# Attention: the third maximum of a step in two 256-key parts, and a bank and an exponential for each score

## The chip, the cores and the metric

The kernel runs on one core of a Trainium2 chip. The time is the device time of one launch in microseconds (us). Three runs of the kernel before gave 3602.53, 3603.29 and 3605.42 us (median 3603.29). A core has TensorE for matmuls (PE in the profile, its weight loads PEld), VectorE (DVE), ScalarE (ACT), GpSimd (POOL) and queues that issue DMAs (SP). Matmuls write to a small memory of eight banks of 512 fp32 columns on 128 partitions (PSUM), which VectorE and ScalarE read.

## The reference

Four sublayers follow each other on x of 2048 tokens by 512: Fourier mixing, attention, Fourier mixing, attention, each on a layer norm of x and added to x. The change lies in the attention:

```python
q = (x @ wq).reshape(B, S, 32, 16).transpose(0, 2, 1, 3)
k = x @ wk                      # one key head of 16 for all 32 query heads
v = x @ wv
scores = einsum("bhqd,bkd->bhqk", q, k) * 16 ** -0.5
p = softmax(scores)
o = einsum("bhqk,bkd->bhqd", p, v)
x = x + o.transpose(0, 2, 1, 3).reshape(B, S, 512) @ wo
```

## The kernel before

**Phases.** A layer has a phase A (Fourier mixing, projections of q, k and v, and some of the maxima early, one after the other between its matmuls) and a phase B (attention and output projection). Phase A of the first layer ends about 644 us into the span and phase B runs to 1801; the second layer's run to 2433 and 3589.

**Rows in halves.** A query or key has 48 rows of values in split precision and rows for the maximum; with padding 64 partitions. Two head groups, g = 0 on partitions 0 to 63 and g = 1 on 64 to 127, share each tile. TensorE is split in two groups of 64 rows, and a matmul of the one can run beside one of the other.

**Phase B** has 512 steps: 16 tiles of 128 queries (`i`), each in 32 steps (`s_`), which are two halves of the heads by 16 chunks of 128 keys. A step does the following.

- `pv` (L910): the probabilities of two steps ago times the values, four matmuls into the one bank z, each on 32 columns of the array and all 128 rows. In the profile these are eight records.
- `score` (L896): four matmuls, j = 0 to 3, g = j mod 2, each 128 keys by 512 (four heads of 128 queries). Two of them fill the two banks of a tile x, and one exponential of 1024 columns (L899) reads both. There are two tiles x, four banks. In the last steps of a layer, when no maxima are left, scores 2 and 3 go to single banks y (L889, L891).
- `max_half` (its matmul shows as L78, its reduce as L102): the softmax needs the maximum of each query and head ahead of its tile's turn. One unit is 128 queries of one head against 512 keys into a bank y, from which VectorE takes one maximum into `mxp`. Units come in the order of (tile, head pair, 512 keys, g), so that g alternates. `owed` holds the pace at three units a step, and twelve ahead.

The banks are z (one), y (three) and x (four). A matmul that takes a bank y waits for the reduce of an earlier one.

**Order.** The program's order is the order on each engine; nothing reorders it. In a step the first unit's g decides: score 1-g, a maximum of g, score g, maxima of 1-g and of g, score 3-g, score 2+g. So one row group gets four matmuls of 512 columns in a step and the other three, and in the next step the other way round. Scores wait for the exponential that read their banks, maxima for the reduces.

**Around it.** Five steps ahead of need, `max_neg` reduces a tile's partial maxima `mxp` (four per head) to `nm`, `max_split` splits it into `ms`, and `max_rows` transposes it and writes it to the rows of q. `out_tasks` and `half_tasks` store, normalise and project the tile before: step 12 of each tile has twelve 128-row matmuls (`o_proj`), and VectorE adds x to the result (L976).

Of the kernel before, what the change touches and what calls it, by code (L numbers as in the profile page):

```python
# [8 lines left out]
F32 = mybir.dt.float32  # L9
# [38 lines left out]
def fnet_mqa_kernel(ctx: ExitStack, tc: tile.TileContext, x_in, ct, dt_, wq, wkv, wo, out):  # L48
# [6 lines left out]
    def f(ap):  # L55
        return ap.bitcast(F32)

# [62 lines left out]

    def pair():
        return ps.tile([P, 2, 512], F32, name="x", bufs=2)
# [127 lines left out]
    def make_layer(L, src, mid, dst, last):  # L250
# [201 lines left out]
        def max_neg(i, p0=0, n=NPAIR, k=4, whole=False):  # L452
            nm = sb.tile([P, NPAIR, 2], F32, name="nm")[:, :n, :]
            vec.tensor_reduce(nm, o.mxp[i][:, p0:p0 + n, :, :k], op=ALU.max, axis=AX.X, negate=True)
            if p0 + n == NPAIR:
                o.mxp.pop(i)
            st["nm"] = nm
            if whole:
                max_split()

        def max_split():
            nmv = st.pop("nm").rearrange("p a g -> p g a")
            n = nmv.shape[2]
            ms = sb.tile([P, 2, 2, NPAIR], F32, name="ms").rearrange("p g r a -> p (g r a)")
            ms = ms[:, :4 * n].rearrange("p (g r a) -> p g r a", g=2, r=2)
# [173 lines left out]
        def phase_a(extra):  # L639
            tasks = {}  # L640
            Pace.pe = Pace.dve = Pace.act = Pace.pool = 0.0
# [212 lines left out]
            units.extend((0, pr, g, 3) for pr in range(HALF, NPAIR) for g in range(2))  # L854
            units.extend((i, pr, g, kb) for i in range(1, NT) for pr in range(NPAIR) for kb in range(4) for g in range(2)
                         if pr >= taken.get((i, kb), 0))
            max_neg(0, 0, HALF, 5, True)
            for k in range(12):
                more_max()
                if k == 2:  # L860
                    max_rows(0, 0, HALF, nc.scalar)

        units = []
        o.done = o.extra = 0

        def more_max():
            if o.done < len(units) and units[o.done][0] in o.loaded | {0}:
                max_half(*units[o.done])
                o.done += 1

        def owed(n):
            return min(3 * (n + 1) + 12 + o.extra, len(units)) - o.done

        def done_with(i, pr):
            return all(u[:2] > (i, pr) for u in units[o.done:])
# [3 lines left out]
        def score(i, s_, j):  # L879
# [6 lines left out]
            w = j // 2  # L886
            if i == NT - 1 and jj == 1 and o.done == len(units):
# [5 lines left out]
            first = "e" not in st  # L893
            if first:
                st["e"] = pair()
            nc.tensor.matmul(st["e"][:, g, :], kz[64 * g:64 * g + KR, c * P:(c + 1) * P],  # L896
                             o.qT[i][64 * g:64 * g + KR, cp:cp + 4, :], start=True, stop=True)
            if not first:
                nc.scalar.activation(ptiles[i, s_][:, 2 * w:2 * w + 2, :], st.pop("e"), AF.Exp, scale=DH ** -0.5)  # L899
# [65 lines left out]
        def o_proj(i):  # L965
            for k in range(NK):
                o_mm(k)
                if k == NK - 1:
                    o_add(i)
                if k % 2 and 3 <= i < NT - 1:  # L970
                    for _ in range(2):
                        more_max()
                        o.extra += 1
# [64 lines left out]
        def phase_b(nxt):  # L1038
# [9 lines left out]
            behind = []  # L1048
            for n in range(NT * NSTEP):
# [4 lines left out]
                g = units[o.done][2] if o.done < len(units) else 1  # L1054
                for j, m in ((1 - g, 1), (g, 2), (3 - g, 0), (2 + g, 1)):
                    score(i, s_, j)
                    for _ in range(m):
                        if owed(n) >= 1:
                            more_max()
# [16 lines left out]
                for at, j, p0, np_ in ((NT - AHEAD, i, HALF, HALF), (NSTEP - AHEAD, i + 1, 0, HALF if i == NT - 2 else NPAIR)):  # L1076
                    if j in (0, NT - 1) or j == i + 1 < NT:
                        if s_ == at:
                            assert done_with(j, p0 + np_ - 1), (n, j, o.done, len(units), units[o.done], owed(n))
# [3 lines left out]
                        if s_ == at + 2:  # L1083
                            max_rows(j, p0, np_)
            if nxt is not None:
# [70 lines left out]
```

## Time and profile before

| what | value |
|---|---|
| runs (us) | 3602.53, 3603.29, 3605.42 |
| the profiled execution's own time | 3602.02 us |
| its span | 3600.2 us |
| granted TensorE clock | 0.997 |
| phase B, layer 1 and 2 | 1157 and 1156 us |
| phase B, busy of 1157.18 us | PE 1150.76, DVE 975.60, ACT 1002.46, POOL 168.10 |

A row of a timeline gives start, length (of all merged instructions together), engine, line, operation, tiles and, in brackets, the idle time before and what ended it. The chain of waits in order of time has start, length and what the end waited on. A group of instructions has line, engine, operation, out<-in, count, busy us, mean ns of one, and idle time with what ended it. A length is from issue to result, so neighbouring instructions of one engine overlap: their spacing, not their length, is what they cost in a row. PE ends are modelled.

### The profile page before, as it was taken

What the parts mean: (1) busy time and instruction counts of PE and PEld (TensorE: products, weight loads), DVE (VectorE), ACT (ScalarE), POOL (GpSimd) and SP (SyncE); (2) the same over time, 40 slices, a digit from 0 to 9 for tenths busy, and PEclk for the clock granted to TensorE, in tenths of its full rate; (3) what the DMA queues carried; (4) which work ended last, traced back from release to release, by engine and by line L of the source; (5) the groups of instructions that cost most, each with busy time, mean ns of one, the idle gap of its engine ahead of it and who ended that gap; (6) DMA issues with size and microseconds to landing.
All of it is one profiled execution on the core that took longest, in us unless ns stands there. A gap on an engine that the chain in (4) does not pass through costs nothing.

```text
span 3600.2 us, 63751 instructions
## 1 busy us (share of the span) xinstructions
PE 3551.6 (99%) x25090; PEld 1901.3 (53%) x25090; DVE 2801.6 (78%) x4819; ACT 2390.8 (66%) x3050; POOL 781.9 (22%) x976
## 2 busy tenths in 40 slices
PE   8999999999999999999999999999999999999999
PEld 6787877434333433343377878773433343333433
DVE  6186987888888888888311979878888888888882
ACT  4323232888888888888933232229888888888888
POOL 5544342011211111111264343420000000000000
PEclk9999999999999999999999999999999999999999
DMA  5544242211111100110144343422111111011100
GB/s 181 140 140 134 99 137 60 75 49 37 34 32 51 34 23 22 49 34 25 40 141 113 128 118 106 130 60 86 34 35 34 50 35 34 22 29 43 35 24 25
DMA packets 204445, 240.85 MB, mean 67 GB/s; under 512 B 36848, under 2 KB 160752, under 8 KB 197232
## 3 DMA queue, kind: packets, MB, share of 16 engines
q1 hardware_dynamic: 199216, 219.98, 20.5%
q0 software_dynamic: 4864, 16.78, 1.6%
q8 instruction: 196, 3.21, 0.4%
q14 instruction: 105, 0.86, 0.1%
q10 hardware_dynamic: 64, 0.02, 0.0%
HBM read 172.48 MB, written 63.17 MB: 65 GB/s over the span
## 4 chain that ended last, share of the span: by engine, by line
PE 85%; DVE 7%; ACT 2%; issue 1%; DMA 1%; SPq 0%; POOL 0%; DVEq 0%; ACTq 0%; POOLq 0%
PE z L910 27%; PE y L78 19%; PE x L896 19%; PE x L78 17%; DVE mxp L102 4%; PE z L78 1%; DVE mxe L102 1%; ACT slot L899 1%; PE z L83 1%; ACT slot L891 0%; PE y L889 0%; DVE row L102 0%; DVE bst L102 0%; DVE ms L102 0%; PE y L83 0%
## 5 line engine op out<-in xcount | busy, mean ns | idle before, releaser
L102 DVE TENSOR_REDUCE mxp<-y 128x1 f32<-128x512 f32 (+1 forms) x3472 | 2166.7, 679 | 267.3 <-PE y L78 218.1
L899 ACT ACTIVATE slot<-x 128x1024 f32<-128x1024 f32 x1992 | 1943.4, 1027 | 313.6 <-PE x L896 226.4
L910 PE MATMUL z<-slot,v 128*32 128x512 f32 x8192 | 1096.4, 605 | 1.7 <-ACT row L913 1.7
L78 PE MATMUL y<-kz,slot 64*128 64x512 f32 (+1 forms) x3048 | 980.1, 424 | 4.4 <-DVE kz L102 2.1
L896 PE MATMUL x<-slot,kz 64*128 64x512 f32 x2960 | 891.2, 447 | 0.8 <-DMA slot<-mt 0.8
L896 PEld LDWEIGHTS x<-slot,kz 64*128 64x128 f32 x2960 | 368.1, 185 | 734.3 <-ACT slot L899 599.7
L78 PEld LDWEIGHTS y<-kz,slot 64*128 64x128 f32 x3048 | 487.8, 185 | 121.8 <-DVE mxp L102 26.5
L78 PE MATMUL x<-ch,xnh 64*128 64x512 f32 (+2 forms) x2048 | 531.6, 372 | 11.7 <-ACT xnh L102 9.5
L78 PE MATMUL x<-ch,xnl 64*128 64x512 f32 (+2 forms) x2048 | 527.8, 364 | 1.0 <-POOL xnl L102 0.6
L78 PE MATMUL x<-cl,xnh 64*128 64x512 f32 (+2 forms) x2048 | 524.3, 364 | 0.4 <-POOL cl L102 0.4
L950 POOL TENSOR_TENSOR row<-row,row 128x256 f32<-128x256 f32 x63 | 46.3, 734 | 1573.7 <-DMA row<-rd 1184.2
L102 POOL TENSOR_TENSOR cl<-craw,ch 128x512 fp32r<-128x512 f32 x244 | 318.0, 1321 | 298.2 <-ACT ch L102 243.0
L78 PEld LDWEIGHTS x<-ch,xnh 64*128 64x128 f32 (+1 forms) x2048 | 293.1, 185 | 63.4 <-issue 16.2
L78 PEld LDWEIGHTS x<-ch,xnl 64*128 64x128 f32 (+1 forms) x2048 | 298.7, 185 | 38.0 <-POOL xnl L102 4.4
L78 PEld LDWEIGHTS x<-cl,xnh 64*128 64x128 f32 (+1 forms) x2048 | 295.0, 185 | 32.2 <-POOL cl L102 0.7
L910 PEld LDWEIGHTS z<-slot,v 128*32 128x32 f32 x8192 | 163.7, 108 | 274.6 <-issue 247.5
L102 ACT COPY junk<-x 128x2 f32<-128x2 f32 x236 | 37.7, 160 | 350.6 <-PE x L78 328.0
L102 DVE TENSOR_REDUCE mxe<-y 128x1 f32<-128x512 f32 x408 | 257.1, 679 | 9.8 <-PE y L78 9.6
L102 ACT CAST ch<-craw 128x512 fp32r<-128x512 f32 x264 | 158.8, 620 | 155.7 <-PE x L78 120.2
L78 PE MATMUL y<-slot,slot 128*128 128x512 f32 x816 | 216.4, 406 | 8.2 <-DVE mxp L102 6.7
L78 PEld LDWEIGHTS y<-slot,slot 128*128 128x128 f32 x816 | 144.7, 188 | 63.1 <-issue 28.2
L896 PE MATMUL x<-xnl,kz 64*128 64x512 f32 x512 | 154.5, 443 | 0.3 <-DMA xnl<-mt 0.3
(126 smaller groups left out, 2576.9 us busy)
## 6 DMA issues: line engine op xcount, KB each, us to landing
craw<-ct_in SPq DMA_DIRECT2D x112, 512.0 KB
slot<-qd SPq DMA_DIRECT2D x42, 1024.0 KB
qd<-row SPq DMA_DIRECT2D x144, 128.0 KB
od<-row SPq DMA_DIRECT2D x252, 64.0 KB
row<-x_in SPq DMA_DIRECT2D x32, 256.0 KB
mid<-row POOLq DMA_DIRECT2D x32, 256.0 KB, 2.6
craw<-ct_in SPq DMA_DIRECT2D x32, 256.0 KB
row<-mid SPq DMA_DIRECT2D x32, 256.0 KB
```

Source lines behind the costliest of these rows:

```text
L78: nc.tensor.matmul(out_, w, x, **k)
L83: nc.tensor.transpose(out_, x, i_)
L102: return fn(out_, in_, *a, **k)
L896: nc.tensor.matmul(st["e"][:, g, :], kz[64 * g:64 * g + KR, c * P:(c + 1) * P], o.qT[i][64 * g:64 * g + KR, cp:cp + 4, :], start=True, sto ...
L899: nc.scalar.activation(ptiles[i, s_][:, 2 * w:2 * w + 2, :], st.pop("e"), AF.Exp, scale=DH ** -0.5)
L910: nc.tensor.matmul(a[32 * j:32 * j + 32, :], v1[:, c, :], pt[:, j, :], start=c == 0, stop=c == NT - 1)
L950: nc.gpsimd.tensor_mul(bt["ot"][:, cs], bt["ot"][:, cs], bt["den"][:, cs])
```

## The change

- A step takes two "whole" units as before (g = 0 and g = 1 of the same 512 keys) and a "couple" in place of a third unit: 256 keys for both g, in the two halves of one y bank. The couple's matmul for g = 0 ("half 0") is the first of the step behind `pv`, that for g = 1 ("half 1") the last. One reduce with two results follows it. A couple exists in 968 of the 1024 steps.
- The two halves write one bank from two row groups, so half 1 waits until half 0 has ended: an empty instruction on ScalarE (`relay`), ahead of score 1's exponential, waits for half 0, and half 1 waits for it.
- Each score has a bank (e0 to e3, one buffer each) and an exponential of 512 columns. Their order is 1, 0, 3, 2, whatever the units are. The four banks are a pool of their own, `scores`, in place of the tiles x, which phase A takes from a pool `pairs`.
- `mxp` has six columns instead of four. The couple of the second 256 keys of a set writes to column 4 or 5. A memset on GpSimd sets these at each tile's start.
- `nm` and `ms` live in a row tile that the attention's output also uses.

The diff, cut to its core:

```diff
...
+    def behind_(later, first):
+        tc.add_manual_dep(later.ins, first.ins.name,
+                          mybir.DependencyInfo(mybir.DependencyClass.Sync, mybir.DependencyReason.DATA), reason="row halves")
...
+    class Wide:
+        cm = pool = None
+
+    def wide(name):
+        if Wide.cm:
+            Wide.cm.__exit__(None, None, None)
+        Wide.cm = name and tc.tile_pool(name=name, bufs=1, space=PSUM, reuse_waits="tile")
+        Wide.pool = name and Wide.cm.__enter__()
+
     def pair():
-        return ps.tile([P, 2, 512], F32, name="x", bufs=2)
...
-                o.mxp[i] = sb.tile([P, NPAIR, 2, 4 if i else 5], F32, name=f"mxp{i % 4}")
+                o.mxp[i] = sb.tile([P, NPAIR, 2, 6], F32, name=f"mxp{i % 4}")
+                nc.gpsimd.memset(o.mxp[i][:, HALF if i == 0 else 0:, :, 4:6], -3.0e38)
...
+        def max_whole(i, pr, kb):
+            for g in range(2):
+                max_half(i, pr, g, kb)
+
+        def max_couple(i, pr, kb, h, g):
+            if g == 0:
+                st["couple"] = bank("y").rearrange("p (g c) -> p g c", g=2)
+            gs = slice(64 * g, 64 * g + KR)
+            c0 = 512 * kb + 256 * h
+            m = nc.tensor.matmul(st["couple"][:, g, :], o.qT[i][gs, pr, :], kz[gs, c0:c0 + 256], start=True, stop=True)
+            if g == 0:
+                st["first"] = m
+                return
+            behind_(m, st.pop("relay"))
+            k = kb
+            if h:
+                k = 4 + o.coupled.get((i, pr), 0)
+                o.coupled[i, pr] = k - 3
+                assert k < 6
+            nc.vector.reduce_max(partial(i)[:, pr, :, k], st.pop("couple"), axis=AX.X)
+
+        def relay():
+            st["relay"] = nc.scalar.nop()
+            behind_(st["relay"], st.pop("first"))
...
-        def max_neg(i, p0=0, n=NPAIR, k=4, whole=False):
-            nm = sb.tile([P, NPAIR, 2], F32, name="nm")[:, :n, :]
+        def max_neg(i, p0=0, n=NPAIR, k=6, whole=False):
+            st["gather"] = half(0 if i or p0 else 2)
+            nm = st["gather"][:, 64:64 + 2 * n].rearrange("p (a g) -> p a g", g=2)
...
+        def pick_whole(n):
+            if owed(n) >= 2 and ready():
+                o.done += 2
+                return pairs.pop(0)
+
+        def pick_couple(n):
+            if owed(n) < 1:
+                return None
+            if "rest" in st:
                 o.done += 1
+                return *st.pop("rest"), 1
+            if ready():
+                o.done += 1
+                st["rest"] = pairs.pop(0)
+                return *st["rest"], 0
...
-            first = "e" not in st
-            if first:
-                st["e"] = pair()
-            nc.tensor.matmul(st["e"][:, g, :], kz[64 * g:64 * g + KR, c * P:(c + 1) * P],
+            e = Wide.pool.tile([P, 512], F32, name=f"e{j}")
...
+            if "first" in st:
+                relay()
+            nc.scalar.activation(ptiles[i, s_][:, j, :], e, AF.Exp, scale=DH ** -0.5)
...
+            wide(f"scores{L}")
             for n in range(NT * NSTEP):
                 i, s_ = divmod(n, NSTEP)
                 if len(behind) == 2:
                     pv(*behind.pop(0))
                 behind.append((i, s_))
-                g = units[o.done][2] if o.done < len(units) else 1
-                for j, m in ((1 - g, 1), (g, 2), (3 - g, 0), (2 + g, 1)):
-                    score(i, s_, j)
-                    for _ in range(m):
-                        if owed(n) >= 1:
-                            more_max()
+                whole = pick_whole(n)
+                couple = pick_couple(n)
+                if couple:
+                    max_couple(*couple, 0)
+                score(i, s_, 1)
+                score(i, s_, 0)
+                if whole:
+                    max_whole(*whole)
+                score(i, s_, 3)
+                score(i, s_, 2)
+                if couple:
+                    max_couple(*couple, 1)
```

TensorE, one step in the middle of phase B. Before (`z` is pv, `x` scores, `y` maxima; the second name is what moves or stays: kz the keys, the other the queries; the bracket names the engine waited for):

```order
L910 MATMUL z_14743<-slot6_14958,v1_74 32x512 x4
L896 MATMUL x_15008<-xnh_85,kz_70 128x512 [waits Activation_49]
L78 MATMUL y_15010<-kz_70,slot0_13547 128x512 [waits DVE_49]
L896 MATMUL x_15008<-xnh_85,kz_70 128x512
L78 MATMUL y_15015<-kz_70,slot0_13547 128x512 [waits DVE_49]
L78 MATMUL y_15018<-kz_70,slot0_13547 128x512 [waits DVE_49]
L896 MATMUL x_15021<-xnh_85,kz_70 128x512 [waits Activation_49]
L896 MATMUL x_15021<-xnh_85,kz_70 128x512
```

and of the change:

```order
L969 MATMUL z_18411<-slot6_18645,v1_74 32x512 x4
L464 MATMUL y_18702<-kz_70,slot1_15927 128x256 [waits DVE_49]
L954 MATMUL e1_18705<-slot8_13907,kz_70 128x512 [waits Activation_49]
L954 MATMUL e0_18709<-slot8_13907,kz_70 128x512 [waits Activation_49]
L82 MATMUL y_18712<-kz_70,slot1_15927 128x512 [waits DVE_49]
L82 MATMUL y_18715<-kz_70,slot1_15927 128x512 [waits DVE_49]
L954 MATMUL e3_18718<-slot8_13907,kz_70 128x512 [waits Activation_49]
L954 MATMUL e2_18721<-slot8_13907,kz_70 128x512 [waits Activation_49]
L464 MATMUL y_18702<-kz_70,slot1_15927 128x256 [waits Activation_sequencer_49]
```

The row groups are, in order behind z, before (here g = 0): 1, 0, 0, 1, 0, 1, 0; now 0, 1, 0, 0, 1, 1, 0, 1. The first maximum of a step stood second and is now fifth, behind half 0 and score 0 of its row group. The banks of y, by the wait counts in the program: before, each of a step's three maxima takes the bank of the maximum with the same place in the step before. Now half 0 takes the bank of whole 0 of the step before, whole 0 that of whole 1, and whole 1 (y_18715) that of the couple (y_18673, next rows); the last is so in 930 steps.

VectorE, the reduces of a step. Before:

```order
L102 TENSOR_REDUCE mxp3_14893<-y_15010 128x1 [waits PE_49]
L102 TENSOR_REDUCE mxp3_14893<-y_15015 128x1 [waits PE_49]
L102 TENSOR_REDUCE mxp3_14893<-y_15018 128x1 [waits PE_49]
```

and of the change, two steps:

```order
L106 TENSOR_REDUCE mxp0_17873<-y_18683 128x1 [waits PE_49]
L106 TENSOR_REDUCE mxp0_17873<-y_18686 128x1 [waits PE_49]
L474 TENSOR_REDUCE mxp0_17873<-y_18673 128x2 [waits PE_49]
L106 TENSOR_REDUCE mxp0_17873<-y_18712 128x1 [waits PE_49]
L106 TENSOR_REDUCE mxp0_17873<-y_18715 128x1 [waits PE_49]
L474 TENSOR_REDUCE mxp0_17873<-y_18702 128x2 [waits PE_49]
```

The couple's bank is the first of the step to be written to and the last to be read.

More of the change, by code (lines that the diff above doesn't have):

```diff
@@ L853, in phase_a, with ready, more_pair @@
                 taken[EARLY[e][:2]] = NPAIR - len(left)
-            units.extend((0, pr, g, 3) for pr in range(HALF, NPAIR) for g in range(2))
-            units.extend((i, pr, g, kb) for i in range(1, NT) for pr in range(NPAIR) for kb in range(4) for g in range(2)
+            pairs.extend((0, pr, 3) for pr in range(HALF, NPAIR))
+            pairs.extend((i, pr, kb) for i in range(1, NT) for pr in range(NPAIR) for kb in range(4)
                          if pr >= taken.get((i, kb), 0))
+            o.total = 2 * len(pairs)
             max_neg(0, 0, HALF, 5, True)
-            for k in range(12):
-                more_max()
-                if k == 2:
+            for k in range(6):
+                more_pair()
+                if k == 1:
                     max_rows(0, 0, HALF, nc.scalar)
[L863 to L868, printed above, removed]
-                o.done += 1
+        pairs = []
+        o.done = o.extra = o.total = 0
+        o.coupled = {}
+        def ready():
+            return pairs and pairs[0][0] in o.loaded | {0}
+        def more_pair():
+            if ready():
+                max_whole(*pairs.pop(0))
+                o.done += 2
+        def pick_whole(n):
+            if owed(n) >= 2 and ready():
+                o.done += 2
+                return pairs.pop(0)
[3 more added lines that the diff above has]
+            if "rest" in st:
+                o.done += 1
+                return *st.pop("rest"), 1
+            if ready():
+                o.done += 1
+                st["rest"] = pairs.pop(0)
+                return *st["rest"], 0
         def owed(n):
-            return min(3 * (n + 1) + 12 + o.extra, len(units)) - o.done
+            return min(3 * (n + 1) + 12 + o.extra, o.total) - o.done
         def done_with(i, pr):
-            return all(u[:2] > (i, pr) for u in units[o.done:])
+            return all(u[:2] > (i, pr) for u in pairs + [st[k] for k in ("rest",) if k in st])
         ptiles = {}
@@ L885, in score @@
                 ptiles[i, s_] = slot((6, 7, 2)[k % 3]).rearrange("p (j n) -> p j n", j=4)
-            w = j // 2
-            if i == NT - 1 and jj == 1 and o.done == len(units):
+            if i == NT - 1 and jj == 1 and o.done == o.total:
                 e = bank("y")
@@ L892, in score @@
                 return
-            first = "e" not in st
-            if first:
-                st["e"] = pair()
-            nc.tensor.matmul(st["e"][:, g, :], kz[64 * g:64 * g + KR, c * P:(c + 1) * P],
+            e = Wide.pool.tile([P, 512], F32, name=f"e{j}")
+            nc.tensor.matmul(e, kz[64 * g:64 * g + KR, c * P:(c + 1) * P],
                              o.qT[i][64 * g:64 * g + KR, cp:cp + 4, :], start=True, stop=True)
-            if not first:
-                nc.scalar.activation(ptiles[i, s_][:, 2 * w:2 * w + 2, :], st.pop("e"), AF.Exp, scale=DH ** -0.5)
+            if "first" in st:
+                relay()
+            nc.scalar.activation(ptiles[i, s_][:, j, :], e, AF.Exp, scale=DH ** -0.5)
         acc = {}
@@ L970, in o_proj @@
                 if k % 2 and 3 <= i < NT - 1:
-                    for _ in range(2):
-                        more_max()
-                        o.extra += 1
+                    more_pair()
+                    o.extra += 2
         def o_add(i):
@@ L1084, in phase_b @@
                             max_rows(j, p0, np_)
+            wide(None)
             if nxt is not None:
```

8 lines of the change are left out of this document (4 added, 4 removed).

## The prediction

> **What bounds the kernel now.** I read the page first, then the chain of waits, then single steps on the timeline.
>
> ```profile
> PE 3551.6 (99%) x25090; PEld 1901.3 (53%) x25090; DVE 2801.6 (78%) x4819; ACT 2390.8 (66%) x3050; POOL 781.9 (22%) x976
> PE 85%; DVE 7%; ACT 2%; issue 1%; DMA 1%; SPq 0%; POOL 0%; DVEq 0%; ACTq 0%; POOLq 0%
> ```
>
> TensorE is busy nearly all the time and carries 85% of the chain. The change touches the attention phase only, 1024 steps in two layers. There the chain, seen in order of time, repeats itself:
>
> ```profile
> 1195.62 1.00 PE z L910 x8
> ...
> 1204.12 0.99 PE z L910 x8
> 1205.11 0.42 PE x L896
> 1205.54 0.00 PE y L78
> 1205.54 0.23 PE x L896
> 1205.77 0.23 PE y L78 x2
> 1206.00 0.24 PE x L896
> ...
> 1212.63 1.00 PE z L910 x8
> ```
>
> From 1195.62 to 1212.63 are eight steps: 2.126 us each. In a step the probability-times-value block takes 0.99 us. Then come the 64-row matmuls, about 0.235 us for 512 columns on one half of the array's rows. Both halves work side by side, but there are seven matmuls, so one half gets four of them. The same on the timeline:
>
> ```profile
> 1201.37 1.89 DVE L102 TENSOR_REDUCE mxp<-y 128x1 f32<-128x512 f32 x3 [0.23 <-PE y L78]
> 1202.93 0.49 PE L896 MATMUL x<-slot,kz 64*128 64x512 f32 x1
> 1202.93 0.49 PE L78 MATMUL y<-kz,slot 64*128 64x512 f32 x1
> 1203.26 0.39 PE L896 MATMUL x<-slot,kz 64*128 64x512 f32 x1
> 1203.31 0.18 PEld L78 LDWEIGHTS y<-kz,slot 64*128 64x128 f32 x1
> 1203.49 1.89 DVE L102 TENSOR_REDUCE mxp<-y 128x1 f32<-128x512 f32 x3
> 1203.62 0.18 PEld L896 LDWEIGHTS x<-slot,kz 64*128 64x128 f32 x2
> 1203.62 0.50 PE L896 MATMUL x<-slot,kz 64*128 64x512 f32 x2
> 1203.75 1.94 ACT L899 ACTIVATE slot<-x 128x1024 f32<-128x1024 f32 x2 [0.18 <-PE y L78]
> 1204.05 1.06 PE L910 MATMUL z<-slot,v 128*32 128x512 f32 x8
> 1205.04 0.49 PE L896 MATMUL x<-slot,kz 64*128 64x512 f32 x1
> ```
>
> First score and first maximum start at 1202.93, the next pair at 1203.26: 0.335 us, since the first weight load has no cover (0.10 over the 0.235). Four places on the busier half make 0.335 + 3 x 0.235 = 1.04; the value block starts 1.12 after 1202.93, so the switch costs 0.08. With the block's 0.99 (1204.05 to 1205.04) TensorE alone gives 2.11, and the step is 2.126: TensorE sets it.
>
> Two engines are close behind. ScalarE needs 1.94 for its two exponentials. VectorE reduces three banks in 1.89, the first starting 0.56 after the first maximum's matmul. The y banks number three. The reduces of the step before end at 1201.37 + 1.89 = 1203.26, and the third maximum's weights load at 1203.31. So that maximum comes only just after its bank is free: release to load is 0.05. This circle goes over two steps: last reduce, 0.05, 0.10 for the load, 0.235 for the maximum, 0.235 for the score behind it, 0.08, 0.99, then the first maximum of the next step but one to its reduce 0.56, then 1.89. Sum 4.14, or 2.07 a step, against 2.126. The slack is 0.06 us.
>
> **The change part by part.**
>
> I call the rows 0 to 63 row group 0 and 64 to 127 row group 1; scores 0 and 2, "whole 0" (a maximum over 512 keys) and "half 0" (256 keys) run on the one, scores 1 and 3, "whole 1" and "half 1" on the other. The two halves fill one bank, the couple's, and share a reduce. So in 968 steps the third maximum, 512 columns on one row group, becomes 256 columns on each. Each then has 3.5 places for 4, if whole 1 may start before whole 0: 0.115 us less, 2.01 a step.
>
> VectorE's work: no fewer reduces; the third writes two columns. The trace has no such form, so I take bounds.
>
> ```profile
> L102 DVE TENSOR_REDUCE mxp<-y 128x1 f32<-128x512 f32 x3408 | 2142.3, 684 | 258.1 <-PE y L78 212.8 <-PE x L896 37.3
> L102 DVE TENSOR_REDUCE mxp<-y 128x1 f32<-128x256 f32 x64 | 24.4, 420 | 9.2 <-PE y L78 5.3 <-PE x L78 1.7
> L102 DVE TENSOR_REDUCE nm<-mxp 128x32 f32<-128x128 f32 x28 | 7.7, 276 | 0.0
> ```
>
> Low 684 ns, as one reduce of 512; high 2 x 420 = 840, as two of 256. By 684 and 420, 128 elements into one result would be 288, and 128 into 32 results take 276: a result more costs nothing. I take 684.
>
> **The order of the reduces is where the change loses.** Until now the first reduce belongs to a matmul that starts with the step. Now VectorE's order is whole 0, whole 1, couple, and whole 0 stands behind half 0 and score 0 on its rows: 0.335 - 0.115 + 0.235 = 0.455 into the step. The couple's reduce is last as before, and its bank is given to whole 1 of the next step (in 930 of the 968 steps, by the program's wait counts), wanted 0.335 into it. With TensorE's 2.01: whole 0 starts at 0.455, its reduce at 0.455 + 0.46 (0.56 without the load's 0.10) = 0.915, all three end at 2.805. Whole 1 of the next step could start at 2.345 and comes, 0.05 behind the bank's release, at 2.855: 0.51 late. Scores 3 and 2, half 1 and the value block stand behind it in TensorE's queue. That a waiting matmul holds back what follows, even on idle rows, shows where the other phase puts a pair of maxima between its matmuls:
>
> ```profile
> 2375.58 0.18 PEld L78 LDWEIGHTS y<-kz,slot 64*128 64x128 f32 x1 [0.79 <-DVE kz L102]
> 2376.04 0.18 PEld L78 LDWEIGHTS y<-kz,slot 64*128 64x128 f32 x1 [0.28 <-DVE kz L102]
> 2376.05 0.29 PEld L78 LDWEIGHTS x<-ch,xnh 64*128 64x128 f32 x2
> ```
>
> The second maximum waits for VectorE until 2376.04. The two loads behind it wait for nothing of their own, and the first of them is for the rows that the first maximum had left; they come at 2376.05.
>
> The lateness feeds back, over two steps. From the couple's last reduce: 0.05, whole 1 with its uncovered load 0.335, score 3 0.235, half 1 0.115, the switch 0.08, the block 0.99, then 0.455 to whole 0, 0.46 to its reduce, 1.89 for three. Sum 4.61: **2.305 us a step**, 0.18 over 2.126. Where whole 1's place in the order matters (before or behind whole 0), it is not in this sum: the wait puts it behind anyway.
>
> How many steps: 968, less two each for the 32 output projections, whose twelve extra matmuls let VectorE catch up.
>
> ```profile
> L976 DVE TENSOR_TENSOR row<-y,row 128x512 f32<-128x512 f32 x32 | 22.1, 692 | 70.6 <-PE y L78 56.2 <-issue 14.4
> ```
>
> 904 x 0.18 = 163 us.
>
> ScalarE: four exponentials of 512 for two of 1024. The end of the phase has both kinds:
>
> ```profile
> 3535.29 1.03 ACT L899 ACTIVATE slot<-x 128x1024 f32<-128x1024 f32 x1 [0.51 <-PE x L896]
> 3536.21 1.08 ACT L891 ACTIVATE slot<-y 128x512 f32<-128x512 f32 x2
> 3537.16 1.04 ACT L899 ACTIVATE slot<-x 128x1024 f32<-128x1024 f32 x1
> ```
>
> and its group on the page by shapes is
>
> ```profile
> L891 ACT ACTIVATE slot<-y 128x512 f32<-128x512 f32 x112 | 67.0, 712 | 0.0
> ```
>
> One of 1024 holds the engine 0.92 us, two of 512 hold it 0.95. Four take 1.90 for 1.84, nothing while a step is 2.30; without that cover 0.06 a step. In the closing steps without maxima, 28 a layer (112 such exponentials by two a step and two layers), ScalarE does set the pace: 1.87 (3535.29 to 3537.16) becomes 1.90, 2 us in all.
>
> The relay adds a wait on half 0, ahead of the exponential of score 1. Half 0 is done some 0.4 into the step, the score's own 0.49, and half 1 is not due before 0.80, so I cost it at nothing. If the empty instruction ended the overlap of neighbouring exponentials, it would cost ScalarE 0.1 of its 0.4 spare. In its queue stand the exponentials, and TensorE's scores wait for these.
>
> Small pieces: 32 memsets on GpSimd, which is 22% busy; between nothing and 0.2 us each (6 us), I take 1. Reading six columns instead of four makes 36 reduces some 0.07 us longer (2 us at most, in VectorE's idle time). The output of that reduce, now in a row tile, waits for stores issued nine steps earlier: nothing. The other phase keeps its order.
>
> Sum against the profiled execution's 3602.02 us (1.8 over its span, 1.3 under the median of the runs): 3602 + 163 + 2 + 1 = 3768, **3768 us**, 4.6% slower.
>
> Bounds of the main case: with whole 1's load covered (0.10 a circle, 0.05 a step) 45 us less, 3720; with the couple's reduce as two (0.16 a circle) 72 us more, and with all 968 steps paying 11 more, 3850.
>
> **The rivals.**
>
> *Faster: the bank is free in time.* The place is whole 1; the point is a couple's reduce that ends within 0.29 us of the next step's start. Then TensorE's 2.01 holds; ScalarE's 1.90 and VectorE's three reduces (1.81 by 1.89 less one overlap of 0.08) fit under it. 968 x 0.115 = 111 us: 3494. For it: each engine's own work is less than 2.01. Against it: 0.51 us would have to come from terms that are all measured.
>
> *Same: no half place is won, and no wait decides.* If matmuls must start in program order, whole 1 cannot start before whole 0, both go at 0.455, and half 1 ends at four places as now: 2.126, so 3604. The Trainium skill, "TensorE: Matmul & The Clock Gate", part 3, "The mechanism", states just that: matmuls start and end strictly in order. No row above settles it, since in today's order no half waits for the other. By that rule alone 3604 would be the time; the bank's wait comes on top, so it gets a small chance.
>
> *Slower still: ScalarE loses its overlap.* If each 512 exponential holds the engine as long as a lone one, as this copy of 512 does,
>
> ```profile
> L913 ACT COPY row<-z 128x512 f32<-128x512 f32 x64 | 38.1, 596 | 1.3 <-PE z L910 1.1
> ```
>
> a step is 4 x 0.6 = 2.4, 0.27 more in 968 steps: 265 us, 3870. Against it: the 0.95 for two above; for it: each now has a wait and a release of its own.
>
> **How the numbers follow.** The main case 0.76, faster 0.10, same 0.06, slower still 0.08. The main case by itself is 3720 to 3850; the range goes from 3690 (a smaller lateness) to 3880 (with ScalarE's case) and leaves out faster and same, 0.16, and little of the main case. A difference under 0.2% (7 us) cannot be told from none here. Faster by more: 0.11, same: 0.05, slower: 0.84.
>
> **What would show it.** In the changed kernel's profile: value blocks 2.30 apart (or in turn about 2.0 and 2.6) instead of 2.126; a row of TensorE's weight loads for y that wait for VectorE's mxp, about 0.2 us a step, where today's are short; VectorE idle some 0.5 us ahead of its first reduce in each step, waiting for TensorE's y; the 128x2 reduce at about 0.68; four exponentials at a spacing of 0.475 with idle time between steps; half 1 without a wait for the relay. I would be wrong if the blocks stand 2.0 apart (the bank is free in time), if they stay at 2.126 with whole 0 and whole 1 always starting together, or if ScalarE has no gap.

## The result and the profile after

The changed kernel takes 3764.58 us (median of four runs, 3763.86 to 3767.84). The kernel before, run beside it, took 3602.91 (3600.57 to 3605.42). The ratio is 1.045, with a 95% interval of 1.0432 to 1.0468: 161.7 us slower. The forecast was 3768.

From the page of the changed kernel, the busy times and three of the costliest groups (busy us, mean ns of one, then the engine's idle us just before, and what ended it):

```profile
PE 3697.4 (98%) x26058; PEld 2085.4 (55%) x26058; DVE 2810.0 (75%) x4819; ACT 2516.9 (67%) x5042; POOL 784.7 (21%) x1008
...
L106 DVE TENSOR_REDUCE mxp<-y 128x1 f32<-128x512 f32 (+1 forms) x2504 | 1588.3, 677 | 420.2 <-PE y L82 386.5
...
L474 DVE TENSOR_REDUCE mxp<-y 128x2 f32<-128x512 f32 x968 | 660.0, 682 | 0.0
...
L82 PEld LDWEIGHTS y<-kz,slot 64*128 64x128 f32 x2352 | 382.3, 185 | 173.8 <-DVE mxp L474 98.6
```

VectorE has about the busy time that it had (2810 us for 2802), ScalarE 126 us more (2516.9 for 2390.8), with twice as many exponentials of half the length. VectorE now stands idle 420 us ahead of its single reduces (267 on the page of the kernel before), and TensorE's weight loads for the whole maxima wait 99 us for the couple's reduce (the loads of the maxima before waited 26.5 us for VectorE). TensorE's 98% is no sign of more work: in the long step below the two maxima's matmuls show as 0.86 us of busy time, while the second of them waits.

The chain of waits of the changed kernel, in order of time, in the stretch in which the values' matmuls are on L969 and the whole maxima on L82:

```profile
1260.11 0.99 PE z L969 x8
...
1261.64 0.70 PE y L82 x2
...
1262.69 0.99 PE z L969 x8
...
1264.23 0.23 PE y L82 x2
...
1264.70 0.99 PE z L969 x8
...
1267.29 0.99 PE z L969 x8
...
1271.88 0.99 PE z L969 x8
```

The value blocks stand 2.58, 2.01 and 2.59 apart, so steps take turns: in the long one the two whole maxima hold the chain for 0.70, in the short one for 0.23. From 1262.69 to 1271.88 are four steps, 2.298 us each. Elsewhere the turns are 2.2 and 2.4, with the same mean.

The same place on the timeline, where the cause can be read:

```profile
1261.11 0.68 DVE L474 TENSOR_REDUCE mxp<-y 128x2 f32<-128x512 f32 x1
1261.48 0.86 PE L82 MATMUL y<-kz,slot 64*128 64x512 f32 x2
1261.84 0.18 PEld L82 LDWEIGHTS y<-kz,slot 64*128 64x128 f32 x1 [0.40 <-DVE mxp L474]
1261.85 0.29 PEld L954 LDWEIGHTS e<-slot,kz 64*128 64x128 f32 x2
...
1262.62 1.06 PE L969 MATMUL z<-slot,v 128*32 128x512 f32 x8
1263.12 0.68 DVE L474 TENSOR_REDUCE mxp<-y 128x2 f32<-128x512 f32 x1
...
1263.61 0.38 PE L464 MATMUL y<-kz,slot 64*128 64x256 f32 x1
...
1263.95 0.50 PE L82 MATMUL y<-kz,slot 64*128 64x512 f32 x2
...
1264.49 1.29 DVE L106 TENSOR_REDUCE mxp<-y 128x1 f32<-128x512 f32 x2 [0.69 <-PE y L82]
...
1265.70 0.68 DVE L474 TENSOR_REDUCE mxp<-y 128x2 f32<-128x512 f32 x1
```

The couple's reduce ends at 1261.79. At 1261.84, 0.05 later, the weights of whole 1 load, after a wait of 0.40 for that reduce; the two loads of the scores stand right behind it at 1261.85. Then come the value block, the next step, VectorE idle for 0.69 until whole 0 is there, and the three reduces, the last of which ends at 1266.38. From 1261.79 to 1266.38 are two steps: 4.59 us. The couple's reduce of the step between (it ends at 1263.80) comes in time for that step's whole 1, and that step is the short one.

For the whole phase, from the first value block of a layer to its last (columns: length, then busy us and instructions of TensorE, its weight loads, VectorE, ScalarE and GpSimd, the granted clock, the DMA share, GB/s):

```profile
644.50:1882.70 1238.20, 1223.53 (x8301) 546.26 (x8299) 981.44 (x1699) 1065.65 (x2077) 169.06 (x358) 1.00 0.12 36
2514.90:3751.90 1237.00, 1223.20 (x8302) 545.13 (x8300) 966.87 (x1609) 1065.37 (x2077) 65.53 (x118) 1.00 0.12 35
```

The kernel before took 1157 and 1156 us between the same two events. The 162 us more lie all in this phase; the clock is 1.00 in it.

### The profile page after: what moved, and what is told of

It reads as the page before. It is cut to its first block, busy times and chain, and to the rows that moved or that the text cites. A ratio compares the mean times of both kernels' runs of the same rounds, so it can differ in the third digit from the quotient of the medians.

```text
span 3763.0 us, 67757 instructions
## 1 busy us (share of the span) xinstructions
PE 3697.4 (98%) x26058; PEld 2085.4 (55%) x26058; DVE 2810.0 (75%) x4819; ACT 2516.9 (67%) x5042; POOL 784.7 (21%) x1008
## 4 chain that ended last, share of the span: by engine, by line
PE 87%; DVE 6%; ACT 2%; issue 1%; DMA 0%; POOL 0%; SPq 0%; DVEq 0%; ACTq 0%; POOLq 0%
PE z L969 26%; PE y L82 20%; PE x L82 17%; PE e L954 12%; PE y L464 10%; DVE mxp L106 3%; PE z L82 1%; DVE mxe L106 1%; ACT slot L951 1%; ACT slot L958 1%; PE z L87 0%; DVE row L106 0%; PE y L949 0%; DVE bst L106 0%; PE y L87 0%
## 5 line engine op out<-in xcount | busy, mean ns | idle before, releaser
L958 ACT ACTIVATE slot<-e 128x512 f32<-128x512 f32 x3984 | 2075.5, 611 | 343.9 <-PE e L954 324.9
L106 DVE TENSOR_REDUCE mxp<-y 128x1 f32<-128x512 f32 (+1 forms) x2504 | 1588.3, 677 | 420.2 <-PE y L82 386.5
L969 PE MATMUL z<-slot,v 128*32 128x512 f32 x8192 | 1096.7, 605 | 0.9 <-ACT row L972 0.9
L954 PE MATMUL e<-slot,kz 64*128 64x512 f32 x2960 | 877.7, 430 | 0.2 <-DMA slot<-mt 0.2
L82 PE MATMUL y<-kz,slot 64*128 64x512 f32 (+1 forms) x2352 | 742.3, 425 | 5.0 <-DVE kz L106 2.1
L474 DVE TENSOR_REDUCE mxp<-y 128x2 f32<-128x512 f32 x968 | 660.0, 682 | 0.0
L464 PEld LDWEIGHTS y<-kz,slot 64*128 64x128 f32 x1392 | 256.4, 184 | 606.6 <-DVE mxp L106 559.2
L82 PE MATMUL x<-ch,xnh 64*128 64x512 f32 (+2 forms) x2048 | 532.9, 372 | 11.9 <-ACT xnh L106 9.8
L82 PE MATMUL x<-ch,xnl 64*128 64x512 f32 (+2 forms) x2048 | 529.1, 364 | 1.5 <-POOL xnl L106 1.1
L82 PE MATMUL x<-cl,xnh 64*128 64x512 f32 (+2 forms) x2048 | 526.2, 364 | 0.4 <-POOL cl L106 0.4
L82 PEld LDWEIGHTS y<-kz,slot 64*128 64x128 f32 x2352 | 382.3, 185 | 173.8 <-DVE mxp L474 98.6
L464 PE MATMUL y<-kz,slot 64*128 64x256 f32 x1392 | 459.0, 330 | 0.0
L954 PEld LDWEIGHTS e<-slot,kz 64*128 64x128 f32 x2960 | 421.6, 185 | 49.4 <-ACT slot L958 45.1
L82 PEld LDWEIGHTS x<-ch,xnh 64*128 64x128 f32 (+1 forms) x2048 | 297.6, 185 | 63.2 <-issue 16.2
L82 PEld LDWEIGHTS x<-ch,xnl 64*128 64x128 f32 (+1 forms) x2048 | 303.2, 185 | 37.4 <-POOL xnl L106 4.8
L82 PEld LDWEIGHTS x<-cl,xnh 64*128 64x128 f32 (+1 forms) x2048 | 299.3, 185 | 31.7 <-POOL cl L106 0.7
L969 PEld LDWEIGHTS z<-slot,v 128*32 128x32 f32 x8192 | 163.6, 108 | 254.9 <-issue 231.7
```

The costliest lines, as they stand in the source:

```text
L82: nc.tensor.matmul(out_, w, x, **k)
L106: return fn(out_, in_, *a, **k)
L464: m = nc.tensor.matmul(st["couple"][:, g, :], o.qT[i][gs, pr, :], kz[gs, c0:c0 + 256], start=True, stop=True)
L474: nc.vector.reduce_max(partial(i)[:, pr, :, k], st.pop("couple"), axis=AX.X)
L954: nc.tensor.matmul(e, kz[64 * g:64 * g + KR, c * P:(c + 1) * P], o.qT[i][64 * g:64 * g + KR, cp:cp + 4, :], start=True, stop=True)
L958: nc.scalar.activation(ptiles[i, s_][:, j, :], e, AF.Exp, scale=DH ** -0.5)
```

## The experiments

The theory is the circle of two steps: the couple's reduce comes last on VectorE and its bank is given to whole 1, so whole 1 is late, and with it all that follows on TensorE. The rivals were that the four single exponentials cost the time, that the half places themselves cost it, or that the order of the maxima alone does not matter.

**Whole 0 first.** The change's parts stay, and only the order within a step is another: whole 0 opens the step, so that VectorE's first reduce can start early, and whole 1 stands as the third of its row group.

```diff
                 couple = pick_couple(n)
+                if whole:
+                    max_half(whole[0], whole[1], 0, whole[2])
+                score(i, s_, 1)
                 if couple:
                     max_couple(*couple, 0)
-                score(i, s_, 1)
+                score(i, s_, 3)
                 score(i, s_, 0)
                 if whole:
-                    max_whole(*whole)
-                score(i, s_, 3)
+                    max_half(whole[0], whole[1], 1, whole[2])
                 score(i, s_, 2)
```

> The changed kernel with another order in a step: whole 0, score 1, half 0, score 3, score 0, whole 1, score 2, half 1. The same instructions, banks and exponentials. My circle: the couple's last reduce, 0.05, whole 1 with its load 0.335, half 1 0.115, the switch 0.08, the value block 0.99, whole 0 at once and its reduce 0.56, three reduces 1.89; sum 4.02, 2.01 a step, the same as TensorE's own 2.01. So 0.29 a step less than the change's 2.30: about 3515 us, faster than both kernels, no weight load of whole 1 waiting for the couple's reduce for long. Rival, the exponentials of 512 (and the relay) are what costs: nothing about them differs, so 3765. Rival, TensorE wins no half place: 2.126, about 3605.

Measured: 3554.89 us (3551.14 to 3558.94, four runs; ratio to the kernel before 0.9867, interval 0.9852 to 0.9881). By the order alone 210 us go, and the kernel is now faster than the one before the change. So the change's matmuls and exponentials are not what cost the time; their order is. But it is 40 us above what was expected: the middle distance between value blocks is 2.07 and not 2.01. Rows of this kernel's timeline (the view merges records that overlap, so ScalarE's are those of narrow windows):

```profile
1258.54 1.10 ACT L958 ACTIVATE slot<-e 128x512 f32<-128x512 f32 x2
...
1259.02 1.18 ACT L958 ACTIVATE slot<-e 128x512 f32<-128x512 f32 x2
...
1259.69 0.18 PEld L954 LDWEIGHTS e<-xnh,kz 64*128 64x128 f32 x1
...
1260.12 1.07 PE L969 MATMUL z<-slot,v 128*32 128x512 f32 x8
...
1261.12 0.50 PE L954 MATMUL e<-xnh,kz 64*128 64x512 f32 x1
...
1261.68 2.07 ACT L958 ACTIVATE slot<-e 128x512 f32<-128x512 f32 x4
...
1263.80 0.18 PEld L954 LDWEIGHTS e<-xnh,kz 64*128 64x128 f32 x1
```

A record of an exponential is about 0.6 long. The third and fourth exponentials of a step start at 1258.54 and 1259.02, 0.48 apart; the first one of the next step follows at 1259.60, 0.58 later, because it waits for score 1. So ScalarE isn't full: its four exponentials need 4 x 0.48 = 1.92, and the rest of the step it waits for TensorE. What sets this step is a second circle over two steps, through the bank of score 2. The last exponential of a step, which reads that bank, ends at 1259.64; the weights of the next score 2 load at 1259.69, 0.05 behind it; score 2, half 1 and the value block follow, the block at 1260.12. Then score 1 of the step after starts at 1261.12, its exponential at 1261.68, and the four end at 1263.75. At 1263.80 the weights of score 2 load again: 4.11 for two steps, 2.06 each. In 838 of the 968 steps of this trace that load stands 0.05 behind the exponential. My sum for this order had no exponential in it. The couple's circle is close behind: whole 1's weights load 0.05 after the couple's reduce here too (1259.42 and 1259.48), but its matmul starts at 1259.60, as early as its row group allows. Two experiments below, with shorter exponentials and with the copy moved, bear on this reading.

**Whole 1 before whole 0.** The changed kernel, with the two whole maxima exchanged. Now whole 0 gets the couple's bank, and whole 1's reduce is first on VectorE.

```diff
         def max_whole(i, pr, kb):
-            for g in range(2):
+            for g in (1, 0):
```

> The changed kernel with whole 1 issued and reduced before whole 0, nothing else. The couple's bank then goes to whole 0, which is due 0.12 later, and the first reduce belongs to whole 1, which starts 0.335 into the step and not 0.455. My circle: 0.05, whole 0 with its load 0.335, score 2 0.235, the switch 0.08, the block 0.99, whole 1 at 0.335, 0.46 to its reduce, 1.89: 4.375, 2.19 a step, so about 3655 us. Rival, matmuls must start in program order and this is what holds the step at 2.30: then the swap frees half a place and the step goes to 2.01, 3500. Rival, the exponentials: 3765.

Measured: 3657.58 us (one run), a middle distance of 2.19 between value blocks. This kernel's view of the waits (total us, times, longest):

```profile
PEld y L82 <- DVE mxp L474: 184.4, 694, 0.4
```

against, in the changed kernel,

```profile
PEld y L82 <- DVE mxp L474: 136.4, 435, 0.4
```

The wait is still there, on more steps, but the circle is shorter by two half places of 0.115: on row group 1 no half stands ahead of its whole maximum, and on row group 0 none stands behind the late one. 4.61 - 0.23 = 4.38 is 2.19 a step, as measured. The sum of a wait in a view does not rank two kernels; the length of the circle does.

**Joined exponentials.** The changed kernel's order, with each score pair back in two banks of one tile and one exponential of 1024, as before the change.

```diff
-            e = Wide.pool.tile([P, 512], F32, name=f"e{j}")
+            w = j // 2
+            if j % 2:
+                st["e"] = Wide.pool.tile([P, 2, 512], F32, name=f"e{w}")
+            e = st["e"]
...
-            nc.scalar.activation(ptiles[i, s_][:, j, :], e, AF.Exp, scale=DH ** -0.5)
+            if not j % 2:
+                nc.scalar.activation(ptiles[i, s_][:, 2 * w:2 * w + 2, :], e, AF.Exp, scale=DH ** -0.5)
```

> The changed kernel with the couple and its order as they are, but the banks of scores 1 and 0, and of 3 and 2, joined in a tile with one exponential of 1024 each. My circle has no exponential in it: 3765, within 10 us. Rival, four exponentials (or the relay among them) hold ScalarE for longer than the step: 3604 to 3700.

Measured: 3763.88 us (one run), the changed kernel's time to 0.02%. Its chain shows the same turns, 2.56 and 2.03:

```profile
1259.52 0.99 PE z L973 x8
...
1262.08 0.99 PE z L973 x8
...
1264.11 1.00 PE z L973 x8
```

In this order the exponentials are hidden, whichever they are.

**Split exponentials alone.** The other half of the same question: the kernel before, with each exponential of 1024 done as two of 512, and nothing else.

```diff
-                nc.scalar.activation(ptiles[i, s_][:, 2 * w:2 * w + 2, :], st.pop("e"), AF.Exp, scale=DH ** -0.5)
+                e = st.pop("e")
+                for k in ((1 - g), g):
+                    nc.scalar.activation(ptiles[i, s_][:, 2 * w + k, :], e[:, k, :], AF.Exp, scale=DH ** -0.5)
```

> The kernel before with two exponentials of 512 in place of each of 1024, nothing else: no couple, the tiles x as before. By my count of ScalarE's work alone (1.90 under 2.126) no change: 3605. Rival: in the kernel before, the second score pair waits for the second exponential of the step before with no slack, a circle over two steps that holds both exponentials once; it grows by 2 x 0.03, so 0.03 a step or 25 to 30 us: 3630. Rival, the exponential of 512 loses its overlap: 2.4 a step, 3870.

Measured: 3661.19 us (3658.25 to 3663.57; ratio 1.0159, interval 1.0142 to 1.0176). The 3605 and the rival's 3630 were too low, the other rival's 3870 far too high. Its timeline:

```profile
1258.86 4.19 ACT L901 ACTIVATE slot<-x 128x512 f32<-128x512 f32 x8 [0.18 <-PE x L896]
1259.16 1.06 PE L912 MATMUL z<-slot,v 128*32 128x512 f32 x8
...
1260.97 0.19 PEld L896 LDWEIGHTS x<-xnh,kz 64*128 64x128 f32 x2 [0.26 <-ACT slot L901]
...
1263.22 3.22 ACT L901 ACTIVATE slot<-x 128x512 f32<-128x512 f32 x6 [0.18 <-PE x L896]
1263.53 1.06 PE L912 MATMUL z<-slot,v 128*32 128x512 f32 x8
```

Eight exponentials take 4.19, then ScalarE waits 0.18 for a score: 4.36 for two steps (1258.86 to 1263.22), 2.18 each, which is what the value blocks show (4.37 from 1259.16 to 1263.53). The wait comes round through a bank: the second score pair of a step loads its weights (1260.97) only when the last exponential of the step before has released its tile, and the value block and the next step's first score pair, for which ScalarE waits, stand behind it. The kernel before reads the same way: the row of its two exponentials in the prediction has 1.94 of work and 0.18 of waiting for TensorE, 2.12, which is its step. So TensorE alone did not set the step before; TensorE's order and this circle through ScalarE were equally long, and 0.06 us a step more on ScalarE showed at once. The size was right in the prediction, 1.90 for 1.84 where nothing covers it: 0.06 on some 1000 steps is 60 us, and 58 came (3661.19 against 3603.22).

**Half the couple's reduce.** The cost of one term of the circle, changed by itself.

```diff
-            nc.vector.reduce_max(partial(i)[:, pr, :, k], st.pop("couple"), axis=AX.X)
+            nc.vector.reduce_max(partial(i)[:, pr, :, k], st.pop("couple")[:, :, :128], axis=AX.X)
...
-            nc.scalar.activation(ptiles[i, s_][:, j, :], e, AF.Exp, scale=DH ** -0.5)
+            nc.scalar.activation(ptiles[i, s_][:, j, :], e, AF.Exp, scale=1e-3)
```

> The changed kernel, but the couple's reduce reads 128 of the 256 columns of each head group: half of the couple's keys are left out of the third maximum, and the scale of the exponential is set small so that the values stay finite. Theory (the circle of two steps through the couple's reduce: whole 1, the half places, value block, whole 0, three reduces): the reduce costs about 0.26 us less, the circle goes from 4.61 to 4.35, 2.17 a step, about 3640 us. Rival (the matmuls or the exponentials of 512 themselves are dearer, the reduce has slack): no change, 3764 us.

Measured: 3649.32 us (one run), 115 us less than the changed kernel; 118 by the theory (0.13 x 904), nothing by the rival. From its chain:

```profile
1264.71 0.99 PE z L969 x8
...
1273.44 0.99 PE z L969 x8
```

Four steps in 8.73, 2.18 each, where the theory had 2.17 (and about 3640 in the text above). What is taken off a reduce for which VectorE seems to have room (it is busy 75% of the span) comes back nearly in full, at half its length a step, as a circle over two steps has it.

**The couple's reduce twice.**

```diff
-            nc.vector.reduce_max(partial(i)[:, pr, :, k], st.pop("couple"), axis=AX.X)
+            for _ in range(2):
+                nc.vector.reduce_max(partial(i)[:, pr, :, k], st["couple"], axis=AX.X)
+            st.pop("couple")
```

> The changed kernel, with the couple's reduce done twice (nothing left out). Theory of the circle: 0.60 to 0.70 us more in 4.6, that is 0.30 to 0.35 a step over 1808 steps in two layers, each step at 2.61 or so: about 4040 us (4000 to 4100). Rival (VectorE has slack of half a microsecond a step that takes it up): VectorE's 1.55 a step becomes 1.9, still below the step: 3764 us.

(The 1808 steps in it are a slip, as in the text on the accumulator's copy below; the estimate of 4040 goes by 904.) Measured: 4159.1 us (one run), 394 more than the changed kernel, and 119 above the theory's figure. The rival, slack on VectorE, is far off. The value blocks no longer take turns; in the chain two steps are 5.39, from 1348.58 to 1353.97, or 2.70 each. The timeline:

```profile
1350.39 1.30 DVE L106 TENSOR_REDUCE mxp<-y 128x1 f32<-128x512 f32 x2
1350.46 0.18 PEld L82 LDWEIGHTS y<-kz,slot 64*128 64x128 f32 x1 [0.54 <-PE y L82]
...
1351.60 1.41 DVE L475 TENSOR_REDUCE mxp<-y 128x2 f32<-128x512 f32 x2
...
1353.13 0.18 PEld L82 LDWEIGHTS y<-kz,slot 64*128 64x128 f32 x1 [0.48 <-PE y L82]
...
1355.85 0.18 PEld L82 LDWEIGHTS y<-kz,slot 64*128 64x128 f32 x1 [0.54 <-PE y L82]
```

From one load of whole 1 to the next but one, 1350.46 to 1355.85, are again 5.39, so the circle holds here too; it is two of its terms that I had too small. The second reduce adds 0.72 (1.41 for the two, 0.69 for one) and not 0.60. And whole 1 loads 0.12 behind the couple's last reduce (1353.01 to 1353.13) and not 0.05: in this kernel the load waits for a matmul of TensorE as well, which the bracket names. With both, the circle is about 0.8 longer than the 4.59 measured above, 0.40 a step, and on 968 steps that is 387 of the 394 us. But VectorE's four reduces, 1350.39 to 1353.01, fill 2.62 of the step's 2.70, where I had written 1.9 without adding them up. The run agrees with the circle, and as a test of it is weaker than the shorter reduce above.

**Whole 0 first, shorter exponentials.** Do the exponentials set the step of the faster order?

```diff
...
-            nc.scalar.activation(ptiles[i, s_][:, j, :], e, AF.Exp, scale=DH ** -0.5)
+            nc.scalar.activation(ptiles[i, s_][:, j, :448], e[:, :448], AF.Exp, scale=DH ** -0.5)
...
```

> The order with whole 0 first, whose time was 3555 us, with each exponential over 448 of its 512 columns; the values' weights of the last 64 columns are taken from others, so that part of the softmax is left out. If ScalarE's four exponentials at 0.51 set its step of 2.07: each about 0.457, the step falls to TensorE's own 2.01, 3495 to 3515 us. If TensorE or VectorE sets it: no change, 3555 us.

Measured: 3506.39 us (one run), 48 less than with full exponentials. Now ScalarE has an open gap in each step:

```profile
1258.34 1.85 ACT L958 ACTIVATE slot<-e 128x448 f32<-128x448 f32 x4 [0.17 <-PE e L954]
...
1260.36 1.85 ACT L958 ACTIVATE slot<-e 128x448 f32<-128x448 f32 x4 [0.17 <-PE e L954]
```

The step is 2.02 (1258.34 to 1260.36), TensorE's 2.01 as the prediction had worked it out. The length of the exponentials was part of what set the step. The text above has that as ScalarE's own work, four at 0.51; but 0.51 is a mean that holds the wait of 0.10 a step, and the rows of the order alone show the circle through score 2's bank instead. Four exponentials now take 1.85 and not 2.07, which makes that circle 3.89, 1.95 a step, less than TensorE's 2.01. The couple's circle has no exponential in it, so it did not set the 2.07. The half place that the change is about comes near the count of places once nothing waits: 94 us less than the kernel before, which took 3600.63 beside it, and the count said 111.

**Whole 0 first, the accumulator's copy on VectorE.** A version that needs no work left out: the copy of the z bank, every 16 steps, moves from ScalarE to VectorE.

```diff
...
-                nc.scalar.copy(oa, a)
+                nc.vector.tensor_copy(oa, a)
...
```

> The order with whole 0 first (3555 us), with the copy of the accumulator (0.47 us each 16 steps) on VectorE in place of ScalarE. If ScalarE sets the step: 0.03 a step less over 1808 steps, some 25 to 50 us, 3505 to 3530 us. If TensorE or VectorE sets it: 3555 us, or more by VectorE's extra work.

Measured: 3546.31 us (3543.55 to 3547.57; ratio to the kernel before 0.9848, interval 0.9832 to 0.9864). That is the best time of the kernels here that leave nothing out, but the interval overlaps with that of the order alone, so the 9 us between them are not settled. The 25 expected by the count are not there. In the view of the waits of this kernel the value block now waits for VectorE's copy:

```profile
PEld z L969 <- DVE row L972: 12.6, 56, 0.4
```

There is one z bank, so the copy stands ahead of the next value block. The estimate of 25 took ScalarE for full. It has 0.10 of waiting in a step, and the circle through score 2's bank has no copy in 15 of 16 steps, so taking the copy away leaves its 4.11 as it was. This is read from the rows, not tested by itself.

**Whole 0 first, joined exponentials.** One exponential of 1024 holds ScalarE a little less than two of 512, so I joined those of each row group.

```diff
...
-            e = Wide.pool.tile([P, 512], F32, name=f"e{j}")
-            nc.tensor.matmul(e, kz[64 * g:64 * g + KR, c * P:(c + 1) * P],
+            if jj == 0:
+                st["e", g] = Wide.pool.tile([P, 2, 512], F32, name=f"e{g}")
+            e = st["e", g]
+            nc.tensor.matmul(e[:, jj, :], kz[64 * g:64 * g + KR, c * P:(c + 1) * P],
...
-            nc.scalar.activation(ptiles[i, s_][:, j, :], e, AF.Exp, scale=DH ** -0.5)
+            if i == NT - 1 and o.done == o.total:
+                nc.scalar.activation(ptiles[i, s_][:, j, :], e[:, jj, :], AF.Exp, scale=DH ** -0.5)
+            elif jj:
+                nc.scalar.activation(ptiles[i, s_][:, g::2, :], e, AF.Exp, scale=DH ** -0.5)
...
```

> The order with whole 0 first (3555 us; step 2.07 there), with scores 1 and 3 in one pair of banks and scores 0 and 2 in the other, and one exponential of 1024 for each pair. If the four single exponentials (0.51 each, 2.04 a step) set the step there: two joined ones take about 2 x 0.95 = 1.90, under TensorE's own 2.01, and the time goes to that of the short exponentials, 3495 to 3520 us. Rival: a score pair now waits for the joined exponential of its row group, which ends later than the single one did, and the order gains nothing: 3555 us or more.

Measured: 3696.25 us (3694.81 to 3697.88; ratio 1.0262, interval 1.0245 to 1.0279). The rival holds: 141 us worse than with single exponentials. In its chain seven steps take 15.57, 2.22 each:

```profile
1257.31 1.07 PE z L974 x8
...
1272.88 1.07 PE z L974 x8
```

and the timeline has ScalarE and TensorE waiting for each other:

```profile
1261.30 1.94 ACT L963 ACTIVATE slot<-e 128x1024 f32<-128x1024 f32 x2 [0.22 <-PE e L956]
...
1263.28 0.18 PEld L956 LDWEIGHTS e<-xnh,kz 64*128 64x128 f32 x1 [0.21 <-ACT slot L963]
...
1263.61 1.94 ACT L963 ACTIVATE slot<-e 128x1024 f32<-128x1024 f32 x2 [0.37 <-PE e L956]
```

ScalarE starts only when the second score of a row group is there, ends at 1263.24, and TensorE's next score for those banks loads at 1263.28. With single exponentials this wait is 35 us in the whole kernel, here 264:

```profile
PEld e L954 <- ACT slot L958: 35.1, 135, 1.2
```

```profile
PEld e L956 <- ACT slot L963: 263.8, 780, 1.6
```

So a bank and an exponential for each score are no ornament. In the changed kernel's order they gain nothing (the joined ones take the same time), but in the order with whole 0 first the gain is lost without them.

## Why the prediction was right

**The circle.** The sum of 4.61 over two steps measured 4.59, 2.298 a step against 2.305. Its terms, in the timeline of the changed kernel: release to load 0.05; from there to the value block, whole 1, score 3, half 1 and the switch, 0.78 (0.765 in the sum); the block 0.99 (1262.62 to 1263.61); whole 0 to its reduce 0.88 (1263.61 to 1264.49; 0.915 in the sum); three reduces 1.89 (1264.49 to 1266.38). Its place in the program was right too: whole 1 waits for the couple's bank, with the scores behind it. Shown to be the cause, and not only to fit, by the order with whole 0 first (210 us back), by the shorter couple's reduce (115 of 118 us), and by the doubled one, once its terms are measured.

**The form of it.** The wait of whole 1's load was forecast as about 0.2 us a step; it is 0.40 in every second one. Of the two forms named for the blocks, blocks 2.30 apart or 2.0 and 2.6 in turn, the second came. The lateness of 0.51 was for every step; in fact it is 0.57 (2.58 against 2.01) in every other one, and nothing in between. For the time only the mean counts.

**The couple's reduce.** Taken as 684 ns, by bounds 684 and 840; it measured 682. The second result costs nothing.

**The half place.** TensorE's 2.01 rested on whole 1 starting ahead of whole 0, which a rival denied by the rule that matmuls start strictly in program order. In the short step of the timeline half 0 and then score 0 go on row group 0. Score 0 has this row, in a window that leaves out the score ahead of it:

```profile
1263.83 0.39 PE L954 MATMUL e<-xnh,kz 64*128 64x512 f32 x1
```

At 0.235 for a place its rows are taken until about 1264.07. The first of the two whole maxima nevertheless starts at 1263.95, and the second 0.12 later (0.50 for two records, 0.40 and 0.39 long). The trace does not name the rows, but the first can only be whole 1, which is the later one in the program. VectorE agrees: idle by then, it starts on whole 0 at 1264.49, just behind the end of the second record (1264.45), where the first had ended at 1264.35. What is said ahead of the prediction, that nothing reorders the program's order, is then true of what waits and not of what starts. So the rule as the Trainium skill, "TensorE: Matmul & The Clock Gate", part 3, "The mechanism", puts it does not hold across row groups here, by 0.12 us; short steps of 2.01 and the 2.02 with the short exponentials say the same. What holds in order is a matmul that waits for a semaphore: behind it everything waits, as 1261.85 shows.

**The exponentials.** I took 0.475 for one of 512, from two that ran between others of 1024 at the end of the phase. Among their like they are 0.48 apart wherever ScalarE does not wait, so the size was right. In the changed kernel a step of 2.30 hides them, and only the closing steps pay:

```profile
1859.73 1.37 ACT L958 ACTIVATE slot<-e 128x512 f32<-128x512 f32 x2
...
1861.69 1.37 ACT L958 ACTIVATE slot<-e 128x512 f32<-128x512 f32 x2
```

1.96 a step, 0.49 for each; before, the middle closing step was 1.90. That is 3 us in all in place of 2. What the prediction lacked is the way in which exponentials come to cost anything: not when their sum fills the step, but through the bank that the last of them releases. For the time of this change it is nothing, since the longer circle covers it; for the rival "faster" it was decisive. Its 3494 asks only that ScalarE's 1.90 fit under 2.01. It does fit, and with full exponentials the kernel still stops at 3555 when the couple's bank is free in time, because the circle through score 2's bank takes 2.06 a step.

**Steps that pay.** 163 us were forecast: 904 steps at 0.18, with two steps for each output projection left out, since VectorE would catch up there. The phases grew by 162 us, but the starts of the value blocks in the two traces, step against step, divide it otherwise. The closing steps have 3 us of it. The 966 steps ahead of them have 159, 0.165 each, and the 28 steps with a projection among these, with the 28 behind them, have 10 us, 0.18 each: they pay like the others. A price of a step a tenth too high and a count of steps nearly as much too low cancel, so that the total came within 2 us is in part luck.

**What bounds the kernel before.** "TensorE sets it" was half of it. The split exponentials show that the circle of score, exponential and bank release was as tight, 2.12. The prediction did not need it, since a longer circle took over.

**The relay.** Costed at nothing. In the changed kernel's view of the waits no row has half 1 waiting for ScalarE. In the order with whole 0 first the exponential behind the relay starts 0.49 after the one ahead of it, where the others start 0.48 apart: the empty instruction doesn't end their overlap. No run leaves the relay out.

## What to carry to other kernels

Where banks go round among several users, write down for each matmul whose bank it takes and when that bank's reader ends; what counts is when the first of a step's readers can start, because the last one's end follows from it. An engine that is busy for 75% can set the pace through such a circle: there a shorter reader pays at once, and a matmul saved on the busier engine pays nothing. Draw the circle for every kind of bank: when the longest one is shortened, the next may lie close behind it, as the one through the scores' banks did here. And where records overlap, read single starts: a mean distance over a row of them can hold waits that no gap shows.

## What the runs showed of the hardware

Two matmuls on different row groups can start against their order in the program, 0.12 us apart here (1263.95 and 1264.07); a weight load that waits for a bank holds up the loads of both row groups (1261.84 and 1261.85). Exponentials of 512 columns that do not wait start 0.48 apart ((2.07 - 0.62) / 3), those of 448 columns 0.43 ((1.85 - 0.56) / 3), while one of 1024 held ScalarE 0.92 in the prediction's rows: two halves cost about 0.04 more than the whole. Splitting it, with nothing else changed, made a kernel 1.6% slower in which ScalarE seemed to have room.
